# Moving five steps in a fused recurrence and MLP kernel: PSUM banks for one chunk, one chunk's states, one weight rounding, two weight sums, one block sum

## The chip, the cores and the metric

The kernel runs on one core of one Trainium2 chip. The metric is the time of one execution on the device in microseconds; the kernel before takes 552.32 us (median of three runs, 552.24 to 554.02). Five engines work side by side, each through its own instructions in order: PE (matmuls; its weight loads are listed as PEld), DVE (elementwise), ACT (activations and copies), POOL (masks, clearing, output stores) and SP (which issues the loads).

## The reference

A gated linear recurrence per batch entry and head, and then an MLP over all tokens, in fp32 results:

```python
for t in range(S):                       # S = 768, B = 4, H = 8, D = 48
    state = alpha[:, :, t, :, None] * state + einsum('bhd,bhe->bhde', k[:, :, t], v[:, :, t])
    y[:, :, t] = einsum('bhd,bhde->bhe', q[:, :, t], state)
x = y.transpose(0, 2, 1, 3).reshape(B * S, H * D)      # 3072 x 384
h = x @ w_in                                           # w_in 384 x 2048
out = (h * (1 / (1 + exp(-h)))) @ w_out                # w_out 2048 x 384
```

The weights arrive as 64-bit floats and are rounded to fp32 inside the kernel.

## The kernel before

The sequence is cut into 24 chunks of 128 tokens (six per batch entry). Chunk n passes through stages. `bring` turns alpha (a), k and q by PE transpositions against the identity: each result fills one PSUM bank. `products` forms on DVE the running products of alpha by scans (L769, L799), scales k into `kp` (L780) and q into `qp` (L806), both read from PSUM. `scores` multiplies kp and qp on PE, ACT copies the result to `g`, POOL masks it (L854), PE transposes kp, and ACT copies that to `kn` (`back`, L890). `values` makes the chunk's y from g and v (and from the old state), which ACT copies to `xt` (L912). `states` multiplies v and kn into one more bank and adds that to the state (for the first four chunks ACT copies it, L931); v's next load on SP waits for it.

PSUM is shared out by pools: three banks `ps_a` for the recurrence, used in turn; three `ps_m` for the products with w_in; two `ps_o` for those with w_out. For chunks 0 to 3 (`n < GB`, GB = 4), k and q are turned into `ps_o` banks (chunk 1 into `ps_m`), and so is q of chunk 6. For the fifth chunk, n = 4, a, k and q all take `ps_a` banks. From chunk 8 on (`NA`), DVE does the turning.

The MLP's work is cut into pieces that `go_on()` takes one at a time from one list, so that PE has work while the recurrence waits. A plain piece (`enter_plain`) is six fp32 matmuls of one half group with w_in, listed as 12 records, and ACT's silu of the bank (L972). The opening up to chunk 4 is written out by hand in `start()`; after that a loop with due times (`fill`) takes pieces. Most instructions named here are kept in the program's order on their engine.

Weight pieces are rounded by `weights`: ACT makes `up` from the low word (L653), DVE makes the value in L669, L671 and L672, and `fetch()` starts a later piece's load on SP. `up` of piece i + 1 is recorded right after L672 of piece i. `w(n)` in `start()` does the w_in pieces up to number n; there are 12, numbered 0 to 11.

Later groups of four chunks use block sums (a Strassen-like scheme). `enter` makes 8 blocks s[0] to s[7] out of 20 products of w_in blocks, in three banks a, b, c; L1007 is the helper line of its DVE sums. `leave` makes each half group's output from seven products with w_out blocks: b11, t1, b21, t2, b22, b12, t4 in that order, into the two `ps_o` banks a and b. Its DVE lines are L1107 (sums of g cells), L1150 and L1152 (u2, the sum that reads bank b after the fourth product), L1116 (an output tile from a bank, stored by POOL) and L1161 (u3). After each product `done()` is called; in the very first `leave` its third call, after the third product, runs `other_differences()`, which makes the last parts of b12 (L635) and of t4 (L636), two operations each.

An audit of all inputs (`seen`, L722 on DVE) runs beside the later groups, fed by loads on SP into a single buffer.

Of the kernel before, what the change touches and what calls it, by code (L numbers as in the profile page):

```python
# [13 lines left out]
ALU = mybir.AluOpType  # L14
# [341 lines left out]
def quotients(  # L356
# [20 lines left out]
    dve, act, gps = nc.vector, nc.scalar, nc.gpsimd  # L377
# [33 lines left out]
    GB = 4  # L411
# [173 lines left out]
    t1, t2, t4 = [wt[:, i] for i in range(3)]  # L585
# [42 lines left out]
                i = slice(2 * i, 2 * i + 2)  # L628
                dve.tensor_tensor(b12[:, i], b22[:, i], b12[:, i], ALU.subtract)

    def other_differences():

        for i in range(4, HF, 2):
            i = slice(i, i + 2)
            tc.keep_in_program_order(dve.tensor_tensor(b12[:, i], b22[:, i], b12[:, i], ALU.subtract))  # L635
            tc.keep_in_program_order(dve.tensor_tensor(t4[:, i], b21[:, i], t2[:, i], ALU.subtract))  # L636

    def weights(which):

        pieces = [
            (w_in[:, t, c : c + 512], moe_w_in[t * 128 : t * 128 + 128, c : c + 512])
            for t, c in pieces_in
        ] if which == 0 else [
            (w_out[:, f, :], moe_w_out[f * 128 : f * 128 + 128, :]) for f in range(NFT)]
        def rounding(bits):
            n = bits.shape[1]
            up = upp.tile([128, 512], I32, name="up")[:, 0:n]  # L650

            tc.keep_in_program_order(
                act.activation(up, bits.bitcast(U32)[:, :, 0], AF.Copy, scale=2.0**-29))  # L653
            return up

        ahead = []
        for i, (dst, src) in enumerate(pieces):
            if not wide:
                act.dma_start(dst, src)
                yield  # L660
                continue
            assert which == 0 or conv_done[0] == n_conv[0]
            bits = coming.pop(0)
            up = ahead.pop() if ahead else rounding(bits)
            if which == i == 0:
                yield
            hi, w = bits[:, :, 1], dst.bitcast(I32)
            tc.keep_in_program_order(
                dve.tensor_scalar(w, hi, 3, 0x3FFFFFFF, ALU.logical_shift_left, ALU.bitwise_and))  # L669
            settled(  # L670
                dve.scalar_tensor_tensor(w, hi, -(1 << 30), w, ALU.bitwise_and, ALU.bitwise_or))  # L671
            settled(dve.tensor_tensor(w, w, up, ALU.add))  # L672
            if i + 1 < len(pieces):
                ahead.append(rounding(coming[0]))
            fetch()
            yield
# [58 lines left out]
    def bring(n, names="akq"):  # L735

        c = ctxs[n]
        sg = seg[0 if late else n % 2]
        ps = c.setdefault("ps", {})

        for name in names:
            if n >= NA:
                if name == "a":
                    turned(c[name], tokens(sg))
                    load(n + 1, "a")
                continue
            if n < GB and name != "a" or n == 6 and name == "q":

                at = "kq".index(name)
                ps[name] = (bank(at) if n == 1 else out_bank(at, 512)).rearrange("p (j c) -> p j c", c=C)  # L750
            else:
                ps[name] = ps_attn()
            if n == 0 and name != "a" or n == 1 and name != "q":
                idle(2)
            for j in range(NP):
                pe.transpose(ps[name][:, j, :], c[name][:, 2 * j : 2 * j + 2, :], ident)
            if name == "a":
                settled(act.copy(tokens(sg), ps[name]))  # L758
# [221 lines left out]
    def enter(grp, pair):  # L980
        g_tiles(grp, pair)
        halves = [gts[grp, h, pair] for h in range(2)]

        s = [halves[o % 2][:, o // 2] for o in range(8)]
        todo = iter(PRODUCTS)

        def new(i):
            return bank(i).rearrange("p (e n) -> p e n", e=2)

        def add(ps, first=False):  # L990
            w, x = next(todo)
            for e in range(2):
                pe.matmul(ps[:, e], lhsT=block_w(w)[:, 2 * pair + e], rhs=block_x(grp, x),
                          start=(first and e == 0), stop=(e == 1), skip_group_check=True)

        def copy(ps, to=None):
            if to is None:
                to = late["part"].tile([128, 2, TB], F32, name="part")
            act.copy(to, ps)  # L999
            return to  # L1000

        def silu(h, i):
            x = halves[h][:, i : i + 2]
            act.activation(x, x, AF.Silu)  # L1004

        def tt(to, a, b, op=ALU.add):
            dve.tensor_tensor(to, a, b, op)  # L1007

        a, b, c = [new(i) for i in range(3)]
        add(a, True)  # L1010
        copy(a, s[6])
        add(b, True)
        copy(b, s[2])
        add(c, True)
        tt(s[6], s[6], copy(c), ALU.subtract)
        yield
        add(c)
        copy(c, s[7])
        add(b)
        copy(b, s[4])  # L1020
        add(a)
        tt(s[7], s[7], copy(a), ALU.subtract)
        yield
        add(a)
        copy(a, s[5])
        add(b)
        copy(b, s[3])
        tt(s[5], s[5], s[3])
        add(c)
        copy(c, s[0])  # L1030
        yield
        add(a)
        tt(s[4], a, s[4])
        b = new(1)
        add(b, True)
        add(b)
        copy(b, s[1])
        yield
        c = new(2)
        add(c, True)  # L1040
        t = copy(c)
        late_2 = (grp, pair) == (4, 0)
        if not late_2:
            tt(s[2], s[2], t, ALU.subtract)
        a = new(0)
        add(a, True)
        tt(s[6], a, s[6])
        if late_2:
            tc.keep_in_program_order(dve.tensor_tensor(s[2], s[2], t, ALU.subtract))
        silu(0, 2)  # L1050
        add(b)
        tt(s[5], copy(b), s[5], ALU.subtract)
        yield
        add(c)
        tt(s[1], c, s[1])
        late_3 = (grp, pair) == (2, 0)
        if not late_3:
            tt(s[3], s[1], s[3], ALU.subtract)
        a = new(0)
        add(a, True)  # L1060
        tt(s[2], a, s[2])
        if late_3:
            tt(s[3], s[1], s[3], ALU.subtract)
        add(b)
        tt(s[7], b, s[7])
        silu(1, 2)
        yield
        add(c)
        combine(s[1], -1, s[1], -1, s[0])
        tt(s[0], c, s[0])  # L1070
        silu(0, 0)
        a = new(0)
        add(a, True)
        tt(s[3], a, s[3])
        silu(1, 0)
        turn.append(turn.pop(0))
        for h in range(2):
            side_by_side(grp, h, pair)
        yield
# [15 lines left out]
    def leave(grp, h):  # L1095
# [26 lines left out]
        steps, passed = iter(range(7)), iter(range(7))  # L1122

        def done():
            if grp == h == 0 and next(passed) == 2:
                other_differences()
            if 2 * grp + h in (1, 2):
                sums_w(2 * grp + h - 1, 4 * next(steps) + 4)

# [90 lines left out]
    def go_on():  # L1220

        nonlocal done
        next(pieces[done][0], None)
        done += 1
# [34 lines left out]
    def start():  # L1259

        nonlocal bridged
        w = lambda upto: convert(0, upto)
        products(0)
        products(1)
        load(NIN)
        next(conv[0])
        scores(0)
        w(1)
        idle(8)
        scores(1)  # L1270
        values(0)
        back(1)
        w(2)
        states(0)
        values(1)
        bridged = 2
        load_v(NV)
        w(3)
        states(1)
        w(4)  # L1280
        bring(2, "a")
        w(5)
        load(NIN + 1)
        load_v(NV + 1)
        go_on()
        bring(2, "kq")
        w(6)
        products(2)
        go_on()
        w(7)  # L1290
        load(NIN + 2)
        go_on()
        go_on()
        scores(2)
        w(8)
        bring(3)
        w(9)
        values(2)
        states(2)
        load_v(NV + 2)  # L1300
        products(3)
        load(NIN + 3)
        w(10)
        go_on()
        w(11)
        go_on()
        scores(3)
        bring(4)
        load(NIN + 4)
        values(3)  # L1310
        bridged = 4
        w(12)
        go_on()
        states(3)
        load_v(NV + 3)
        products(4)
        side_by_side(0, 0, 0)
        convert(1, 1)
        for _ in range(3):
            convert(1, 3 * (done - 6) // 2)  # L1320
            go_on()
        stated.pop()
        stated.append(False)
# [110 lines left out]
```

## Time and profile before

| | |
|---|---|
| median of three runs | 552.32 us |
| profiled execution, time / span | 552.89 / 551.1 us |
| PE busy | 541.0 us, 98% of the span |
| PE weight loads (PEld) busy | 494.0 us, 90% |
| DVE, ACT, POOL busy | 445.9, 209.0, 80.8 us |
| DMA | 70.11 MB, mean 127 GB/s |

The profile lists one execution. The busy time of an engine is the sum of its instructions; in the timeline, a row gives start and length in us, engine, source line, operation, output<-input by the program's tile names, and how many instructions were merged. What stands in brackets is the engine's idle time just before, and what released it. Ends of matmuls are modelled, weight loads are pulled ahead of running matmuls, so I read PE's standstills from the starts of weight loads.

### The profile page before, as it was taken

To read this page: it belongs to the slowest core of one execution; us is meant where nothing else is said; L and a number is where in the kernel's file an instruction comes from. 1 tells how busy PE (TensorE), PEld (TensorE's weight loads), DVE (VectorE), ACT (ScalarE), POOL (GpSimd) and SP (SyncE) were. 2 spreads that over 40 slices of the span, in tenths; PEclk is the share of its full clock that TensorE was granted. 3 is DMA by queue.
4 is the path that set the end of the run, shared out by engine and by line. 5 is a ranking of instruction groups with operands and counts; after the bars stand their busy time and mean duration, and the time that the engine had idled before them with its cause. 6 is when DMAs were issued, how large, how long until landed. Compare 5 with 4: busy or idle time off the path is not lost. (4 is left out here: it accounts for less than half of the span.)

```text
span 551.1 us, 12716 instructions
## 1 busy us (share of the span) xinstructions
PE 541.0 (98%) x5068; PEld 494.0 (90%) x5068; DVE 445.9 (81%) x801; ACT 209.0 (38%) x466; POOL 80.8 (15%) x146
## 2 busy tenths in 40 slices
PE   8899999999999999999999999999999999999996
PEld 8787888988999899899999999998898999999996
DVE  5999789887988899997998986998884796955531
ACT  3655553223333334344354253253263342332200
POOL 4111001221122102111011021021131000001000
PEclk9999999999999999999999999999999999999999
DMA  9999761355354434445445653717742135500000
GB/s 216 305 237 220 201 187 36 89 138 147 99 132 131 124 84 118 127 132 156 122 121 148 183 140 103 198 33 173 183 132 87 54 94 168 168 19 15 17 26 29
DMA packets 99218, 70.11 MB, mean 127 GB/s; under 512 B 56272, under 2 KB 88656, under 8 KB 99152
## 3 DMA queue, kind: packets, MB, share of 16 engines
q1 hardware_dynamic: 97232, 65.30, 45.4%
q0 software_dynamic: 1920, 3.93, 2.1%
q8 instruction: 41, 0.67, 0.5%
q14 instruction: 25, 0.20, 0.1%
HBM read 61.34 MB, written 7.86 MB: 126 GB/s over the span
## 5 line engine op out<-in xcount | busy, mean ns | idle before, releaser
L394 PE MATMUL ps_o<-w_out,g 128*128 128x192 f32 x768 | 134.0, 329 | 0.8 <-DVE u L1150 0.6
L394 PEld LDWEIGHTS ps_o<-w_out,g 128*128 128x128 f32 x768 | 125.8, 190 | 3.7 <-DVE u L1150 0.9
L394 PE MATMUL ps_m<-xt,w_in 128*128 128x256 f32 x480 | 112.1, 382 | 0.9 <-ACT xt L912 0.5
L394 PEld LDWEIGHTS ps_m<-xt,w_in 128*128 128x128 f32 x480 | 89.8, 190 | 13.9 <-DVE g L1007 0.9
L394 PE MATMUL ps_o<-wt,g 128*128 128x192 f32 x576 | 99.7, 327 | 0.0
L394 PEld LDWEIGHTS ps_o<-wt,g 128*128 128x128 f32 x576 | 95.2, 190 | 1.5
L394 PE MATMUL ps_m<-xc,w_in 128*128 128x256 f32 x288 | 70.8, 382 | 0.0
L394 PEld LDWEIGHTS ps_m<-xc,w_in 128*128 128x128 f32 x288 | 53.8, 190 | 6.9 <-DVE g L1007 0.3
L1004 ACT ACTIVATE g<-g 128x1024 f32<-128x1024 f32 x32 | 33.1, 1056 | 65.5 <-DVE g L1007 65.4
L1107 DVE TENSOR_TENSOR g<-g 128x512 f32<-128x512 f32 x72 | 49.4, 697 | 8.0 <-PE ps_o L394 7.9
L866 POOL TENSOR_SCALAR_AFFINE_SELECT g<-g 64x256 f32<-64x256 f32 x64 | 37.7, 589 | 123.6 <-ACT g L859 104.6
L1119 POOL DMA_DIRECT2D out_dram<-o x40 | 22.0, 550 | 215.3 <-DVE o L1116 111.6
L999 ACT COPY g<-ps_m 128x512 f32<-128x512 f32 x64 | 36.9, 586 | 41.4 <-PE ps_m L394 41.3
L394 PE MATMUL ps_m<-xc,wx 128*128 128x256 f32 x192 | 50.0, 383 | 0.0
L1007 DVE TENSOR_TENSOR g<-ps_m,g 128x512 f32<-128x512 f32 x56 | 37.1, 681 | 3.2 <-PE ps_m L394 2.7
L394 PEld LDWEIGHTS ps_m<-xc,wx 128*128 128x128 f32 x192 | 35.3, 190 | 3.9 <-issue 0.4
L769 DVE TENSOR_TENSOR_SCAN u<-al,one 128x516 f32<-128x516 f32 x24 | 29.7, 1236 | 7.7 <-ACT al L758 7.4
L972 ACT ACTIVATE g<-ps_m 128x512 f32<-128x512 f32 x32 | 19.0, 595 | 37.7 <-PE ps_m L394 37.3
L799 DVE TENSOR_TENSOR_SCAN p<-al,inv 128x516 f32<-128x516 f32 x24 | 30.0, 1248 | 1.0 <-PE ps_a L394 0.3
L722 DVE TENSOR_REDUCE seen<-bits 128x1 f32<-128x512 int32 (+1 forms) x33 | 26.2, 820 | 4.9 <-DMA bits<-in_moe_w_in_dram 4.9
L1116 DVE TENSOR_TENSOR o<-ps_o,u 128x192 f32<-128x192 f32 x24 | 8.5, 353 | 26.8 <-PE ps_o L394 24.9
L999 ACT COPY part<-ps_m 128x512 f32<-128x512 f32 x32 | 18.8, 589 | 25.6 <-PE ps_m L394 21.2
(137 smaller groups left out, 657.3 us busy)
## 6 DMA issues: line engine op xcount, KB each, us to landing
bits<-in_moe_w_in_dram SPq DMA_DIRECT2D x24, 512.0 KB, 5.1
bits<-in_moe_w_out_dram SPq DMA_DIRECT2D x16, 384.0 KB, 3.8
at<-in_alpha_dram SPq DMA_DIRECT2D x64, 96.0 KB, 2.5
kt<-in_k_dram SPq DMA_DIRECT2D x64, 96.0 KB, 2.6
qt<-in_q_dram SPq DMA_DIRECT2D x64, 96.0 KB, 2.6
bits<-in_alpha_dram SPq DMA_DIRECT2D x9, 512.0 KB, 4.0
out_dram<-o POOLq DMA_DIRECT2D x40, 96.0 KB, 2.2
flips<-turn SPq DMA_DIRECT2D x12, 256.0 KB, 2.4
```

The source lines that it names most:

```text
L394: in_order(nc.tensor.matmul(*args, **kw))
L722: dve.tensor_reduce(seen[kind][which][:, i : i + 1], x, axis=AX, op=op, apply_absolute_value=True))
L769: settled(dve.tensor_tensor_scan(u[:, end - 1 :: -1], sg[:, end:0:-1], one[:, end:0:-1], 0.0, ALU.mult, ALU.add))
L799: settled(dve.tensor_tensor_scan(p[:, 0:end], sg[:, 0:end], iv[:, 0:end], 0.0, ALU.mult, ALU.add))
L866: gps.affine_select(x, x, pattern=[[0, NP], [1, CH]], compare_op=ALU.is_ge, fill=0.0, base=0, channel_multiplier=-1)
L972: settled(act.activation(gts[grp, h, pair][:, i : i + 2, q % 2, :], ps, AF.Silu))
L999: act.copy(to, ps)
L1004: act.activation(x, x, AF.Silu)
L1007: dve.tensor_tensor(to, a, b, op)
L1107: dve.tensor_tensor(cells(grp, h, pair, *to), cells(grp, h, pair, *x), cells(grp, h, pair, *y), ALU.subtract)
L1116: dve.tensor_tensor(o, x, y, ALU.add)
L1119: (gps if grp < NG - 1 else nc.sync).dma_start(out[r : r + C, c * HO : (c + 1) * HO], o)
```

## The change

```diff
-    def other_differences():
+    def other_differences(which):
         for i in range(4, HF, 2):
             i = slice(i, i + 2)
-            tc.keep_in_program_order(dve.tensor_tensor(b12[:, i], b22[:, i], b12[:, i], ALU.subtract))
-            tc.keep_in_program_order(dve.tensor_tensor(t4[:, i], b21[:, i], t2[:, i], ALU.subtract))
+            tc.keep_in_program_order(
+                dve.tensor_tensor(b12[:, i], b22[:, i], b12[:, i], ALU.subtract) if which == 0 else
+                dve.tensor_tensor(t4[:, i], b21[:, i], t2[:, i], ALU.subtract))
...
-            if i + 1 < len(pieces):
+            if i + 1 < len(pieces) and (which, i) != (0, 10):
                 ahead.append(rounding(coming[0]))
...
-            if n < GB and name != "a" or n == 6 and name == "q":
+            if n <= GB and name != "a" or n == 6 and name == "q":
...
-        late_3 = (grp, pair) == (2, 0)
+        late_3 = (grp, pair) in ((2, 0), (4, 0))
         if not late_3:
             tt(s[3], s[1], s[3], ALU.subtract)
         a = new(0)
         add(a, True)
         tt(s[2], a, s[2])
         if late_3:
             tt(s[3], s[1], s[3], ALU.subtract)
...
         def done():
-            if grp == h == 0 and next(passed) == 2:
-                other_differences()
+            at = next(passed)
+            if grp == h == 0 and at in (2, 3):
+                other_differences(at - 2)
...
         bring(4)
         load(NIN + 4)
+        w(12)
         values(3)
         bridged = 4
-        w(12)
-        go_on()
         states(3)
         load_v(NV + 3)
+        go_on()
         products(4)
```

In the order of the built kernel this moves the following and nothing else. On PE, k and q of chunk 4 are turned into `ps_o` banks, and the 16 matmuls of states(3) come before one plain piece instead of behind it. On ACT, `up` of w_in piece 11 goes from before a silu to behind the copy of chunk 4's alpha (L758), and the two state copies of chunk 3 come before that piece's silu. On DVE, the two L636 sums go from between the L635 sums to behind L1152, ahead of the next chunk's k transposition; in group 4's first pair the sum s[3] goes behind the sum s[2]; and one L1090 sum (side_by_side) moves by one place among the w_out roundings. On POOL and SP the order is the same as before.

## The prediction

> **What bounds the kernel now.** I read the engine totals first, then the 40 slices, then the timeline of TensorE's weight loads (PEld), which shows every place where the matmul stream stops, and last DVE at those places. The totals:
>
> ```profile
> PE 541.0 (98%) x5068; PEld 494.0 (90%) x5068; DVE 445.9 (81%) x801; ACT 209.0 (38%) x466; POOL 80.8 (15%) x146
> ```
>
> PE is busy for 541.0 of 551.1 us, and the slices show it full in all but the first and the last. The chain of waits is of no use here: it ends at its last instruction. The sum of PEld's waits tells more: nearly all are "issue" gaps of 0.2 to 0.33 us where a run of 128-column loads gives way to narrow ones. So time is won only where PE itself stands still, and work on another engine counts only if PE waits for it. The change touches three places.
>
> First place, w_in matmuls while chunks are prepared. Start, duration, engine, line, operation, out<-in, count, and in brackets the idle time before:
>
> ```profile
> 36.28 0.69 PEld L394 LDWEIGHTS ps_a<-g,vn 128*32 128x32 f32 x26 [0.29 <-POOL g L854]
> ...
> 37.62 5.05 PEld L394 LDWEIGHTS ps_m<-xt,w_in 128*128 128x128 f32 x24
> 42.99 0.97 PEld L394 LDWEIGHTS ps_a<-p,kp 48*128 48x128 f32 x16 [0.33 <-issue]
> ...
> 46.80 0.80 PEld L394 LDWEIGHTS ps_a<-g,vn 128*32 128x32 f32 x28 [0.20 <-POOL g L854]
> 47.79 2.46 PEld L394 LDWEIGHTS ps_m<-xt,w_in 128*128 128x128 f32 x12 [0.20 <-issue]
> 50.58 0.41 PEld L394 LDWEIGHTS ps_a<-vn,kn 128*32 128x32 f32 x32 [0.33 <-DVE p L799]
> 51.06 7.64 PEld L394 LDWEIGHTS ps_m<-xt,w_in 128*128 128x128 f32 x36
> 59.03 0.97 PEld L394 LDWEIGHTS ps_a<-p,kp 48*128 48x128 f32 x16 [0.33 <-DVE w_out L669]
> ```
>
> The lines from 46.80 are the fourth chunk: its y, one w_in piece (12 loads), its states at 50.58, three w_in pieces. Between states and y lies a piece, so the array changes from wide to narrow loads twice (0.20 + 0.33 us). The lines from 36.28 are the third chunk, where states follow y at once: no gap before 37.62.
>
> Second place, the first group's w_out products:
>
> ```profile
> 109.84 0.55 DVE L636 TENSOR_TENSOR wt<-w_out,wt 128x384 f32<-128x384 f32 x1
> ...
> 110.77 0.99 DVE L636 TENSOR_TENSOR wt<-w_out,wt 128x384 f32<-128x384 f32 x1
> ...
> 112.68 2.63 PEld L394 LDWEIGHTS ps_o<-w_out,g 128*128 128x128 f32 x16
> ...
> 115.79 0.36 DVE L1150 TENSOR_TENSOR u<-ps_o,u 128x192 f32<-128x192 f32 x1
> 116.20 2.57 PEld L394 LDWEIGHTS ps_o<-w_out,g 128*128 128x128 f32 x16 [0.89 <-DVE u L1150]
> ```
>
> The sixth product adds into the bank that L1150 still has to read. DVE is late with L1150, and PE stands for 0.89 us, its longest wait behind the start-up.
>
> Third place, group 4, first pair:
>
> ```profile
> 392.56 0.78 PEld L394 LDWEIGHTS ps_m<-xc,w_in 128*128 128x128 f32 x4
> 394.06 0.73 PEld L394 LDWEIGHTS ps_m<-xt,w_in 128*128 128x128 f32 x4 [0.72 <-DVE g L1007]
> ...
> 397.08 2.57 PEld L394 LDWEIGHTS ps_o<-w_out,g 128*128 128x128 f32 x16 [0.49 <-DVE o L1116]
> ```
>
> ```profile
> 392.12 0.69 DVE L722 TENSOR_REDUCE seen<-bits 128x1 f32<-128x512 int32 x1 [1.04 <-DMA bits<-in_moe_w_in_dram]
> 392.72 0.68 DVE L1007 TENSOR_TENSOR g<-g 128x512 f32<-128x512 f32 x1
> 393.32 1.28 DVE L1007 TENSOR_TENSOR g<-ps_m,g 128x512 f32<-128x512 f32 x2
> ...
> 396.70 0.33 DVE L1116 TENSOR_TENSOR o<-ps_o,u 128x192 f32<-128x192 f32 x1
> ```
>
> DVE waits for a transfer, then runs without a break to L1116; PE waits for it twice.
>
> **What the Trainium skill says.** "Perfetto Trace Analysis", Identifying the Most-Contended Engine: matmul busy time flatters, LDWEIGHTS share is the better measure. Here it is 90% beside 98%, and I count gaps in weight loads. "TensorE: Matmul & The Clock Gate", Step-by-step: what each phase is for: matmuls stay in program order, only weight loads are pulled ahead; the trace agrees (115.23 to 116.20 nothing else is put in). "PSUM — Partial Sum Buffer", Specifications (TRN2): eight banks of 2 KiB. The kernel's pools hold 3 + 3 + 2, so two w_out banks are the only spare ones. "SBUF — State Buffer", SBUF: two separate sides: a DVE operation with two SBUF inputs and a GpSimd one lock each other out; the trace agrees, L636 at 110.77 takes 0.99 instead of 0.55 us under an affine_select.
>
> **The change, part by part.**
>
> Chunk 4's k and q into w_out banks, states(3) behind values(3). No instruction is added or removed on PE. Before, the third ps_a bank that states(3) needs was k's, held until DVE had formed kp (48.54 + 0.68 = 49.22); after, it is that of kn, copied out by ACT at 45.81, before y ends. So no wait comes in. The price is read from the third chunk: y to w_in is 37.62 - 36.28 = 1.34 us with states included. A run of 24 loads to the next narrow one takes 42.99 - 37.62 = 5.37, of 36 takes 59.03 - 51.06 = 7.97, so 48 take 10.57. After: 1.34 + 10.57 = 11.91; before: 59.03 - 46.80 = 12.23. Gain **0.32 us** (0.2 to 0.5). It needs its cover: w_out banks are free (q of chunk 3 was read by DVE at 40.41, the next w_out use is q of chunk 6 at 82), and y's start is set by the POOL selects (ended 46.75), which do not move. On ACT states' two copies come before the piece's silu instead of after; on SP the v load behind states keeps its place in the queue and can only start sooner.
>
> Last w_in rounding later. ACT's `up` of piece 11 (0.70 us at 43.02) moves behind the copy of al (45.68 + 0.62 = 46.30); with it on ACT the silu at 43.62 comes some 0.4 us sooner, which PE does not wait for. DVE's L669 and L671 stay; L672 (46.39 before) now waits until about 47.0, ending 47.7 instead of 47.29. Behind it on DVE are the products of chunk 4 and the w_out roundings: all 0.44 us later. Who waits? PE's third w_in matmul of the piece, which after the change comes at about 46.80 + 1.34 + 4 x 0.21 = 49.0, so 1.2 us of cover; scores(4) at 58.7, whose q is ready by 51.8; ACT, whose w_out roundings wait for DVE's L672 (1.00 us at 60.18) and hold up silu and copies behind them. There the ps_a bank for chunk 5's a must be free at about 62.55 and would be at 62.1. DVE's own idle time before 64.51, 2.81 us, swallows the delay. The piece's fetch on SP keeps its place; it was issued at 49.41, behind a load of q. Cost **0** (0 to +0.3).
>
> t4's two sums later. They go from ahead of L1150 to behind L1152. Before, they take 110.31 - 109.84 = 0.47 and 111.68 - 110.77 = 0.91 us of DVE's time, so L1150 comes 0.94 to 1.38 us earlier, at 114.41 to 114.85, ending by 115.21 at the latest. Weight loads of a 16-run follow each other at 2.55 us (110.13 to 112.68), so PE can go on at 115.23. Gain 116.20 - 115.23 = **0.97 us** (0.8 to 1.0). What is late next: the sums' 0.94 us now lie before the k transposition and the store L1116 at 117.47, which frees the bank of the seventh product. It comes 0 to 0.44 us earlier, ending at 117.82 at worst; PE asks for it at 118.74 - 0.97 = 117.77. The sums are done by 116.1, before that product needs them. DVE's waits of 0.64 (119.10) and 1.08 us (123.81) catch the rest.
>
> s[3] behind s[2] in group 4, pair 0. The first of the two sums from 393.32 goes to 392.72, and a's bank is free 0.60 us earlier: PE goes on at 393.46 instead of 394.06. But L1116 at 396.70 stands behind the same DVE work in either order, ends at 397.03, and PE waits for it: 0.49 becomes 1.09 us. Gain **0** (0 to 0.6).
>
> Nothing in PEld's waits after 400 us is more than an issue gap, and DVE, POOL and DMA follow PE's shift, so both gains reach the end. Sum: 0.32 + 0.97 = 1.29 us. The profiled execution took 552.89 us (span 551.1), 0.57 above the median 552.32; it should become 551.6, and the median **551.0**.
>
> **Rivals.**
> A second gain in group 4: DVE's 1.04 us wait for the transfer shrinks or goes. Then L1116 is up to 1.04 us earlier and the waits of 0.65 (394.06 against 393.41) and 0.49 us shrink too: up to 1.14 us more, 549.9 to 550.5. For it: the length of a transfer is not fixed. Against: its issue at 386.96 is tied to DVE's previous reduction, so it moves with the rest.
> Only one gain lands: DVE's 0.44 us after 47 delays ACT near 60, or L1116 near 117.8 costs what L1150 gave: 551.4 to 552.0.
> The other side, slower: the late rounding. Its place is ACT's queue behind al. Each us that `up` comes later than 48.2 holds PE at the piece's third matmul, and through L672 and ACT's roundings near 60 holds the ps_a banks once DVE is more than about 0.9 us late. It decides against the change when that loss passes 1.3 us, so with DVE some 2.2 us late: 552.3 to 554.5. Against: in the built order ACT has nothing but copies of finished tiles before it.
>
> **How the numbers follow.** Main case 0.53 at 551.0 (550.3 to 551.6, as medians of three scatter by tenths); second gain 0.22; one gain only 0.15; slower side 0.10. A measurement tells about 0.3%, 1.66 us, from no change, so faster means below 550.66: the second gain and 0.20 of the main case, 0.42. Slower by that much is 0.07 of the last case; the rest, 0.51, is within. The range 549.9 to 552.2 leaves out most of the slower side and tails.
>
> **What would show it.** Right: no 12-load run between y and states near 47, scores(4) about 0.3 us earlier; no wait at L1150 and PE 1.3 us earlier from 117 on; the wait for L1116 near 396 at about 1.1 us. Wrong: a PE wait for w_in near 49 or for ps_a near 62, a wait for L1116 near 117, or no longer wait near 396.

## The result and the profile after

The changed kernel takes **551.9 us** (median of 14 runs, 551.36 to 553.28) against 552.77 us (14 runs, 551.96 to 554.02) of the kernel before on the same chip: ratio 0.9983, 95% interval 0.9975 to 0.9991. It is faster by 0.17%: the interval leaves out no change, but the size is below the 0.3% that the prediction called distinguishable. The profiled execution took 552.26 us, span 550.5. Lines below line 628 move by one or two: L1007 is now L1008, L1116 L1117, L1150 L1152, L722 L723.

The first table of the page after:

```profile
PE 539.8 (98%) x5068; PEld 493.0 (90%) x5068; DVE 446.3 (81%) x801; ACT 209.1 (38%) x466; POOL 79.7 (14%) x146
```

First place, timeline of the weight loads of the kernel after (start, duration, idle time before in brackets):

```profile
46.69 0.69 PEld L394 LDWEIGHTS ps_a<-g,vn 128*32 128x32 f32 x26 [0.31 <-POOL g L855]
...
47.38 0.58 PEld L394 LDWEIGHTS ps_a<-vn,kn 128*32 128x32 f32 x30
48.02 10.23 PEld L394 LDWEIGHTS ps_m<-xt,w_in 128*128 128x128 f32 x48
58.58 0.97 PEld L394 LDWEIGHTS ps_a<-p,kp 48*128 48x128 f32 x16 [0.33 <-DVE w_out L672]
```

States follow y without a gap, and four w_in pieces come in one run of 48 loads. From y to scores(4) it is 58.58 - 46.69 = 11.89 us, before 12.23: **0.34 us** won.

Second place, DVE and weight loads around the sixth and seventh product, kernel after:

```profile
108.92 1.02 DVE L636 TENSOR_TENSOR w_out<-w_out 128x384 f32<-128x384 f32 x2
...
114.14 0.36 DVE L1152 TENSOR_TENSOR u<-ps_o,u 128x192 f32<-128x192 f32 x1
...
114.87 1.02 DVE L637 TENSOR_TENSOR wt<-w_out,wt 128x384 f32<-128x384 f32 x2
...
116.77 0.34 DVE L1117 TENSOR_TENSOR o<-ps_o,u 128x192 f32<-128x192 f32 x1
```

```profile
112.23 5.23 PEld L394 LDWEIGHTS ps_o<-w_out,g 128*128 128x128 f32 x32
117.43 2.63 PEld L394 LDWEIGHTS ps_o<-wt,g 128*128 128x128 f32 x16
```

The wait of 0.89 us is gone: the fifth and sixth product make one run of 32 loads. From the fifth to the seventh it is 5.20 us, before 118.74 - 112.68 = 6.06: **0.86 us** won. The store sum at 116.77 ends 0.3 us before PE asks for its bank, so nothing takes the place of the wait here.

PE is now 118.74 - 117.43 = 1.31 us ahead: the two gains, and 0.11 us that this execution was ahead before the change begins. In front of group 4 it is 1.36 (372.64 against 374.00). After group 4 it is 0.78 (399.10 against 399.88), and so it stays to the last product (542.55 against 543.33). **0.58 us were given back in group 4.** There, weight loads and DVE of the kernel after:

```profile
387.05 0.73 PEld L394 LDWEIGHTS ps_m<-xt,wx 128*128 128x128 f32 x4 [0.60 <-DVE g L1008]
388.61 0.73 PEld L394 LDWEIGHTS ps_m<-xt,w_in 128*128 128x128 f32 x4 [0.83 <-ACT part L1000]
...
392.83 0.84 PEld L394 LDWEIGHTS ps_m<-xt,w_in 128*128 128x128 f32 x4
...
396.30 2.57 PEld L394 LDWEIGHTS ps_o<-w_out,g 128*128 128x128 f32 x16 [0.84 <-DVE o L1117]
```

```profile
373.87 1.28 DVE L723 TENSOR_REDUCE seen<-bits 128x1 f32<-128x512 int32 x2 [1.84 <-DMA bits<-in_moe_w_in_dram]
...
379.14 1.43 DVE L800 TENSOR_TENSOR_SCAN p<-al,inv 128x516 f32<-128x516 f32 x1
...
391.36 0.69 DVE L723 TENSOR_REDUCE seen<-bits 128x1 f32<-128x512 int32 x1 [0.81 <-DMA bits<-in_moe_w_in_dram]
...
395.91 0.34 DVE L1117 TENSOR_TENSOR o<-ps_o,u 128x192 f32<-128x192 f32 x1
```

The wait of 0.72 us for s2 is gone. In its place are a wait of 0.60 for another sum of g, which the kernel before did not have, and two that are 0.35 longer: 0.83 instead of 0.48 for `part`, 0.84 instead of 0.49 for the store sum. 0.60 + 0.35 + 0.35 - 0.72 = 0.58. All three depend on DVE (`part` is a bank that ACT copies out behind its L1005, and that waits for DVE's g), and DVE begins this stretch by waiting for a piece of w_in that the audit loads. The same stretch before:

```profile
374.61 1.28 DVE L722 TENSOR_REDUCE seen<-bits 128x1 f32<-128x512 int32 x2 [1.24 <-DMA bits<-in_moe_w_in_dram]
...
379.88 1.23 DVE L799 TENSOR_TENSOR_SCAN p<-al,inv 128x516 f32<-128x516 f32 x1
```

The load of that piece was issued at 370.40 before and at 369.07 after, 1.33 us sooner. The reduction that needs it starts only 0.74 us sooner. These are single executions. Against this same trace of the kernel before, the four other kernels that hold the t4 edit and the opening's (described below) lost 0.49 (e8), 0.25 (e4), 0.11 (e9, the same kernel again) and 0.05 us (e12) in group 4, read at the same two points; 0.58 is the largest of the five.

### The profile page after: what moved, and what is told of

It reads as the page before. It is cut to its first block, busy times and chain, and to the rows that moved or that the text cites. A ratio compares the mean times of both kernels' runs of the same rounds, so it can differ in the third digit from the quotient of the medians.

```text
span 550.5 us, 12714 instructions
## 1 busy us (share of the span) xinstructions
PE 539.8 (98%) x5068; PEld 493.0 (90%) x5068; DVE 446.3 (81%) x801; ACT 209.1 (38%) x466; POOL 79.7 (14%) x146
## 5 line engine op out<-in xcount | busy, mean ns | idle before, releaser
L1005 ACT ACTIVATE g<-g 128x1024 f32<-128x1024 f32 x32 | 33.1, 1056 | 66.1 <-DVE g L1008 66.0
L1000 ACT COPY g<-ps_m 128x512 f32<-128x512 f32 x64 | 36.9, 586 | 41.4 <-PE ps_m L394 41.3
L1008 DVE TENSOR_TENSOR g<-ps_m,g 128x512 f32<-128x512 f32 x56 | 37.3, 683 | 3.2 <-PE ps_m L394 2.7
L800 DVE TENSOR_TENSOR_SCAN p<-al,inv 128x516 f32<-128x516 f32 x24 | 30.2, 1260 | 0.9 <-PE ps_a L394 0.2
L723 DVE TENSOR_REDUCE seen<-bits 128x1 f32<-128x512 int32 (+1 forms) x33 | 26.3, 824 | 5.4 <-DMA bits<-in_moe_w_in_dram 5.4
L1117 DVE TENSOR_TENSOR o<-ps_o,u 128x192 f32<-128x192 f32 x24 | 8.5, 354 | 26.7 <-PE ps_o L394 24.8
L1000 ACT COPY part<-ps_m 128x512 f32<-128x512 f32 x32 | 18.9, 589 | 26.0 <-PE ps_m L394 21.0
```

Source lines behind the costliest of these rows:

```text
L723: dve.tensor_reduce(seen[kind][which][:, i : i + 1], x, axis=AX, op=op, apply_absolute_value=True))
L800: settled(dve.tensor_tensor_scan(p[:, 0:end], sg[:, 0:end], iv[:, 0:end], 0.0, ALU.mult, ALU.add))
L1117: dve.tensor_tensor(o, x, y, ALU.add)
```

## The experiments

Edits are against the kernel before or after, as said; each ratio is to the kernel before on the same chip. The first four take the change apart. Where an edit adds or removes lines, later line numbers move with it.

**e1_t4_alone**, the kernel before with the split of `other_differences` and

```diff
+            at = next(passed)
+            if grp == h == 0 and at in (2, 3):
+                other_differences(at - 2)
```

> The kernel before with only t4's two sums moved behind the sum that reads bank b. Theory (each gain is local and additive, group 4 gives part back through the audit's transfer): the 0.89 us wait near 116 goes, the product after it starts 0.86 us earlier; of that 0.4 to 0.9 us reaches the end. Rival (the change gains only through group 4's swapped sums): the wait goes and the end moves by less than 0.2 us.

Measured: 552.29 against 553.02 us, ratio 0.9985 (0.9979 to 0.9991). Its weight loads:

```profile
112.44 5.23 PEld L394 LDWEIGHTS ps_o<-w_out,g 128*128 128x128 f32 x32
117.64 2.30 PEld L394 LDWEIGHTS ps_o<-wt,g 128*128 128x128 f32 x14
```

5.20 us again: this edit alone takes the wait away, 0.86 us.

**e2_start_alone**, the kernel before with the opening's three edits:

```diff
+            if i + 1 < len(pieces) and (which, i) != (0, 10):
...
+            if n <= GB and name != "a" or n == 6 and name == "q":
...
+        w(12)
         values(3)
         bridged = 4
-        w(12)
-        go_on()
         states(3)
         load_v(NV + 3)
+        go_on()
```

> The kernel before with only the opening changed: chunk 4's k and q in w_out banks, chunk 3's states right behind its y, last w_in rounding later. Theory: scores of chunk 4 0.34 us earlier (y to scores 11.89 instead of 12.23 us), 0.1 to 0.35 us at the end, the 0.89 us wait near 116 stays. Rival: DVE's 0.4 us lateness takes it back near 60, nothing at the end.

Measured: 552.59 us, 0.9994 (0.9987 to 1.0002). From y to scores(4) 57.78 - 45.88 = 11.90, and the wait of 0.89 at L1150 stays. At the end of the program this edit alone is not told from no change. By the ratios e1 and e2 add up to 0.21% or 1.2 us.

**e3_swap_alone**, the kernel before with `late_3 = (grp, pair) in ((2, 0), (4, 0))`:

> The kernel before with only s[3] behind s[2] in group 4's first pair. Theory: PE's 0.72 us wait near 394 goes, the wait for the store sum near 397 grows from 0.49 to about 1.1 us, the end moves by less than 0.2 us. Rival: 0.5 us or more is gained at the end.

Measured: 552.95 us, 1.0001 (0.9993 to 1.0008). The wait for s2 goes, that for the store sum becomes 0.60.

**e4_no_swap**, the kernel after with `late_3 = (grp, pair) == (2, 0)`:

> The changed kernel without the swap of s[3] and s[2]. Theory: the same time as the changed kernel within 0.2 us (about 0.9 us under the kernel before); the 0.7 us wait for s[2] is back, the wait for the store sum is about 0.5 us again. Rival (the swap carries the gain): 0.5 us slower than the changed kernel.

Measured: 551.93 us, 0.9980 (0.9973 to 0.9987). A wait of 0.24 for s2 and one of 0.51 for the store sum, together 0.75, where the kernel after has 0.84 at one place. The swap moves a wait and removes none.

The next four ask about the audit's load, the banks and the rounding. **e5_no_audit_load**, the kernel after; **e6_no_audit_load_before** is the same edit on the kernel before. Eleven loads of w_in pieces are left out, the reductions all read the first:

```diff
+            if kind == 1 and landed and todo[at - 1][2] == 1 and at < alone:
+                landed.append(landed[-1])
+                return
```

> The changed kernel in which the audit's DVE reductions of w_in all read the first piece of w_in again; the other 11 w_in loads of the audit are left out (so w_in is audited only in part), the DVE work is the same. Theory (the transfer's landing sets DVE's chain in group 4 and so PE's waits): no DVE wait before the reductions near 374 and 391, PE's waits near 387, 389 and 396 fall from 0.60, 0.83 and 0.84 us to the 0.2 to 0.3 us of ordinary gaps, the end 1.2 to 2 us earlier than the changed kernel. Rival (DVE's own work is the bound there): the waits stay, less than 0.4 us.

> The kernel before with the same audit loads left out as in e5_no_audit_load. Theory (group 4 gives back a part of the two gains because the transfer does not move with PE): between this kernel and e5_no_audit_load lie the full 1.2 us of the two gains, against 0.9 us with the loads. Rival (the loss has another cause): again 0.9 us or less.

Measured: e5 553.12 us, 1.0002 (0.9994 to 1.0010); e6 554.50 us, 1.0024 (1.0015 to 1.0032), beside 553.29 of the kernel before. My expectation of a faster kernel failed: without the loads the reductions come at other places in DVE's order, and other waits come. Weight loads of e5 in group 4 (L1011 is L1008 there, L1003 is L1000), and then two lines of e6:

```profile
372.72 0.81 PEld L394 LDWEIGHTS ps_a<-g,vn 128*32 128x32 f32 x32 [0.23 <-issue]
...
387.82 0.73 PEld L394 LDWEIGHTS ps_m<-xt,wx 128*128 128x128 f32 x4 [1.30 <-DVE g L1011]
389.38 0.73 PEld L394 LDWEIGHTS ps_m<-xt,w_in 128*128 128x128 f32 x4 [0.83 <-ACT part L1003]
...
396.44 2.57 PEld L394 LDWEIGHTS ps_o<-w_out,g 128*128 128x128 f32 x16 [0.20 <-issue]
399.24 0.75 PEld L394 LDWEIGHTS ps_a<-p,kp 48*64 48x64 f32 x32 [0.23 <-issue]
```

```profile
373.92 0.81 PEld L394 LDWEIGHTS ps_a<-g,vn 128*32 128x32 f32 x32 [0.23 <-issue]
...
400.44 0.66 PEld L394 LDWEIGHTS ps_a<-p,kp 48*64 48x64 f32 x30 [0.23 <-issue]
```

The pair answers another question. e6 is at 373.92 where e5 is at 372.72, and at 400.44 where e5 is at 399.24: a lead of 1.20 in front of group 4 and behind it. PE still waits there, 1.30 and 0.83 us in both, for DVE's own sums, but these move with PE: with no load in group 4 **nothing is given back**, and the medians differ by 1.38 us. The 13 runs of each lie within 0.81 and 0.53 us; with the loads, sets of 12 to 15 runs spread over 1.0 to 2.4 us. That is a hint of the loads' scatter and no proof.

**e7_k_q_in_ps_a**, the kernel after with `n < GB` instead of `n <= GB`, so chunk 4's k and q are back in `ps_a`:

> The changed kernel with chunk 4's k and q in ps_a banks again, chunk 3's states still right behind its y. Theory (the w_out banks are what lets the states move): the states wait for DVE's kp, until about 49.5, PE stands for some 2 us, and the kernel is about 2 us slower than the changed one, 1 us slower than before. Rival (the order alone is worth it): the same as the changed kernel.

Measured: 552.35 us, 0.9984 (0.9978 to 0.9991). Its weight loads near 47:

```profile
46.84 0.80 PEld L394 LDWEIGHTS ps_a<-g,vn 128*32 128x32 f32 x28 [0.22 <-POOL g L855]
48.49 0.41 PEld L394 LDWEIGHTS ps_a<-vn,kn 128*32 128x32 f32 x32 [0.85 <-ACT xt L913]
48.97 10.23 PEld L394 LDWEIGHTS ps_m<-xt,w_in 128*128 128x128 f32 x48
59.52 0.64 PEld L394 LDWEIGHTS ps_a<-p,kp 48*128 48x128 f32 x10 [0.33 <-DVE w_out L670]
```

States wait 0.85 us for ACT's copy of y, so 12.68 instead of 11.89 us. The bank that states takes must be y's own: k's is read by DVE only from 48.89 on (L781) and q's later still, behind the start of states at 48.49, and there are three. So the wait expected here, some 2 us for kp, did not come, and the kernel is still faster than the one before, by 0.16%, and 0.5 us slower than e8 on the same chip.

**e8_rounding_early**, the kernel after with `if i + 1 < len(pieces):` as before:

> The changed kernel with the last w_in rounding made ahead again, as before. Theory: DVE's last w_in sum some 0.4 us sooner, PE unmoved, the time of the changed kernel within 0.2 us. Rival (the late rounding carries a part of the gain): 0.3 us or more slower than the changed kernel.

Measured: 551.86 us, 0.9974 (0.9966 to 0.9982). From y to scores(4) 58.42 - 46.51 = 11.91 us. In the time at the end the late rounding costs and brings nothing. Ahead of y it does something that this measure leaves out:

```profile
45.05 0.42 PEld L398 LDWEIGHTS ps_a<-ident,an 128*128 128x128 f32 x4 [1.26 <-ACT g L854]
```

PE waits 1.26 us for ACT's copy of g, 0.37 in the kernel after: in e8 `up` waits on ACT for a rounding of DVE until 43.35 and stands ahead of that copy. So y comes 4.24 us behind scores(3) instead of 3.81, and the same is seen in e1 and e6, which round early too and also reach scores(3) by 42.4 us. By 120 us nothing of it is left (120.13 in e8; 120.08 in e4, which rounds late and reached scores(3) at 42.34).

The last four look at group 4 once more. **e9_changed_again** is the kernel after, unchanged:

> The changed kernel once more, as the zero point of this batch. Both theories: 0.8 to 1.3 us faster than the kernel before, PE 1.3 us ahead of it up to group 4 and about 0.8 us ahead from there, DVE waiting there for the piece of w_in that L711 fetches.

Measured: 551.62 against 552.66 us, 0.9979 (0.9970 to 0.9987). Its waits in group 4 are 0.36, 0.83 and 0.60, and its last product starts at 542.00.

**e10_audit_slots_1_3** and **e11_audit_slots_0_3**, the kernel after with the audit's steps (places in the main loop at which a reduction is put into DVE's order) moved:

```diff
-        if at % 2 == 0 and step > 3 * GB + 2:
+        if at % 2 == 1 and step > 3 * GB + 2:            # e10
+        if at % 4 in (0, 3) and step > 3 * GB + 2:       # e11
```

> The changed kernel with the audit's reductions (L723) put at steps 1 and 3 of every four instead of 0 and 2; nothing is left out. Theory: the changed kernel loses 0.58 us in group 4 because a reduction waits there for its load, with the sums of g and the store sum L1117 queued behind it on DVE. With other steps the wait lies elsewhere in DVE's order, the PE waits for g (0.60), part (0.83) and o (0.84) in group 4 change, and the end comes 0.3 to 1.0 us before that of the changed kernel. Rival: the waits of group 4 come from DVE's own sums and not from the load: the end is within 0.2 us of the changed kernel, or later where the reduction is put ahead of another sum that PE needs.

> The changed kernel with the audit's reductions at steps 0 and 3 of every four; nothing is left out. Theory: the reductions are spread differently, the time from a load's issue to the reduction that uses it grows by a step for one of two, and where that is more than 5 us, DVE no longer waits for it; the end comes 0.2 to 0.8 us before the changed kernel's. Rival: within 0.2 us of it, or later.

Measured: 552.89 us, 1.0002 (0.9994 to 1.0009), and 553.03 us, 1.0005 (0.9997 to 1.0014), both slower than e9. In e10 DVE waits for no load any more, and all three PE waits of group 4 are gone. But the reductions now stand ahead of other sums, of which xc (sums of blocks of x) are the first. DVE and weight loads of e10, a little earlier:

```profile
361.12 1.26 DVE L723 TENSOR_REDUCE seen<-bits 128x1 f32<-128x512 int32 x2
362.31 0.40 DVE L596 TENSOR_TENSOR xc<-xt 128x256 f32<-128x256 f32 x1
```

```profile
363.50 0.73 PEld L394 LDWEIGHTS ps_m<-xc,wx 128*128 128x128 f32 x4 [0.93 <-ACT u L1142]
364.56 0.73 PEld L394 LDWEIGHTS ps_m<-xc,w_in 128*128 128x128 f32 x4 [0.34 <-DVE xc L598]
365.49 0.73 PEld L394 LDWEIGHTS ps_m<-xc,wx 128*128 128x128 f32 x4 [0.19 <-DVE xc L600]
```

1.46 us of waits before matmuls that read xc (the first is put down to ACT, which ended at 363.22; DVE's second sum of xc ends at 363.39), and the last product starts at 542.45 (e11: 542.55), as in the kernel after. In e11 no reduction of group 4 waits for its load either, but DVE then stands 2.09 us for the chunk's alpha (L734, at 375.48), whose load SP issued behind the audit's, at 371.40, and which landed 4.0 us later; PE waits 0.70 us for g and 1.15 us for `part`. The gain sought isn't there: where these waits go, others come to about the same end. That both still end later lies behind the last product, and the last section shows it.

**e12_two_edits**, the kernel after with the early rounding and without the swap:

> Of the change only two parts: chunk 4's k and q in w_out banks with states(3) behind values(3), and t4's last two sums behind L1152. The rounding stays early and s[3] stays ahead of s[2]. Theory: these two carry all of it: within 0.2 us of the changed kernel, 0.8 to 1.4 us faster than the kernel before. Rival: the other two edits carry a part that neither showed alone: 0.3 us or more slower than the changed kernel.

Measured: 551.44 us, 0.9980 (0.9971 to 0.9988). Two of the edits, the opening's order with its banks and the t4 sums, carry all of the change.

**What sets the end.** In ten kernels the audit reads in the same steps and its loads are kept. In each of them I took four times: when the load in front of group 4 is issued, how long it takes until its reduction starts, the same for the next load that DVE waits for (386.43 in the kernel after; the one between them lands well before its reduction), and the start of the last product's weight loads. The rest is what remains.

| kernel | issue | load 1 | load 2 | rest | last product |
|---|---|---|---|---|---|
| before | 370.40 | 4.21 | 5.16 | 163.56 | 543.33 |
| e3 | 370.39 | 4.43 | 4.67 | 163.55 | 543.04 |
| after | 369.07 | 4.80 | 4.93 | 163.75 | 542.55 |
| e9 (after) | 368.95 | 4.63 | 4.66 | 163.76 | 542.00 |
| e8 | 369.24 | 4.79 | 4.88 | 163.74 | 542.65 |
| e4 | 369.16 | 4.77 | 4.67 | 163.75 | 542.35 |
| e12 | 369.17 | 4.60 | 4.55 | 163.84 | 542.16 |
| e1 | 369.30 | 4.75 | 4.64 | 163.74 | 542.43 |
| e2 | 369.90 | 4.61 | 4.78 | 163.79 | 543.08 |
| e7 | 370.05 | 4.60 | 4.85 | 163.77 | 543.27 |

The start of the last product is the issue plus two transfers plus a rest that is the same to 0.1 us in eight kernels and 0.2 us shorter in two. So in group 4 **the loads, with DVE's work between them, set how far PE has come**, and PE's lead counts only as far as it moves the issue. Behind group 4 nothing is lost or won any more: from the scores there to the last product it is 143.45 us before and after (543.33 - 399.88, 542.55 - 399.10), and the same to 0.01 in the other twelve. Of the lead of 1.33 us at the issue, the two transfers took 9.73 - 9.37 = 0.36 and the rest 0.19 us: 0.78.

The 0.19 lies in DVE's work from the first reduction to the second issue: 386.43 - 373.87 = 12.56 us after, 386.96 - 374.61 = 12.35 before. Its cause is in POOL's selects beside DVE's scan. POOL of the kernel after, and then of the kernel before:

```profile
378.89 2.84 POOL L867 TENSOR_SCALAR_AFFINE_SELECT g<-g 64x256 f32<-64x256 f32 x4 [10.16 <-ACT g L860]
```

```profile
380.25 2.49 POOL L866 TENSOR_SCALAR_AFFINE_SELECT g<-g 64x256 f32<-64x256 f32 x4 [10.16 <-ACT g L859]
```

After, the selects begin at 378.89, ahead of the scan L800 at 379.14, and the scan takes 1.43 us. Before, they begin at 380.25, behind the scan's start at 379.88, and it takes 1.23. In the eight kernels with the longer rest the selects come first and the scan takes 1.43 to 1.48; in the two with the shorter rest they come second and it takes 1.23. That is the lock of which the prediction quoted the Trainium skill ("SBUF — State Buffer", SBUF: two separate sides): the one that starts first has the port. Before, the first of the four selects takes 1.06 us, where the last takes 0.41, and ends 0.21 us behind the scan. The selects follow PE, which is 1.36 us earlier; DVE follows the load, which is 0.74 us earlier; so they changed places.

## Why the prediction was right and where not

The median was predicted at 551.0 and came to 551.9. That is inside the whole range of 549.9 to 552.2, but outside the main case (550.3 to 551.6) and inside the range of the rival "only one gain lands". That the number fits the range is so in part luck: the traces show both gains, and what was lost was lost elsewhere. Of the 0.9 us, 0.45 are in the starting point: three runs gave 552.32 for the kernel before, 14 gave 552.77. The gain was put at 1.29 and measured at 0.87 here. The five kernels that hold both edits that count (after, e4, e8, e9, e12) have ratios from 0.9974 to 0.9983, on average 0.9979, which is **1.15 us**, near the 1.29.

- **The opening**: predicted 0.32, measured 0.34. Right in size, wrong in one reason. I had the third bank of states(3) as that of k, held until DVE's kp at 49.22. e7 shows a wait for y's copy and none for kp: the bank would be y's own, and the banks are worth 12.68 - 11.89 = 0.79 us in this order.
- **The late rounding**: predicted 0, and e8 shows 0 at the end. That `up` also stood ahead of ACT's copy of g, for which PE waits, was not seen: it was worth 0.43 us ahead of y in e8, of which nothing is left by 120 us. DVE did wait (L673 at 46.79, 0.65 us for `up`), but the operation took 0.69 instead of 0.90 us, so the scan behind it came 0.19 instead of 0.44 us later (0.30 counted from y). Nothing near 60 waited.
- **The t4 sums**: predicted 0.97, measured 0.86. L1152 came at 114.14, early enough; the term that was mis-sized is PE's pace once nothing stops it, 2.60 us from product to product and not 2.55. The cover that I doubted held: L1117, feared to end at 117.82, ended at 117.11 in a trace that is 0.45 us ahead here, 0.32 us before PE asked.
- **The swap in group 4**: predicted 0, and e3 and e4 show 0. The wait for the store sum was to be 1.1 and is 0.84 and 0.60 (after, e9). In the kernel after PE had stood 0.95 us longer in the two waits ahead of it; in e3, where no lead had to be absorbed, it is 0.60, with DVE's second load 0.49 us shorter than before.
- **"DVE, POOL and DMA follow PE's shift, so both gains reach the end"** is the step that failed. The issue did move, by 1.33 us. But from there the end hangs on two transfers, whose sum was between 9.10 and 9.73 us in the ten kernels above, and POOL followed PE while DVE followed the load, which cost 0.2 us. With those terms the gain is 0.34 + 0.86 - 0.20 = 1.0 us, give or take the transfers. Whether the kernel before always has its selects behind the scan is not known; the two traces that hold neither gain (before, e3) have.
- **The rivals**: the second gain in group 4 did not come, DVE's wait for the first load grew from 1.24 to 1.84 us and the loss was on this side. A single gain is excluded by the weight loads of e1 and e2, which show one gain each where the kernel after shows both; the slower case by the time itself and by e8.
- **The reading of the weight loads' waits**: "nearly all" issue gaps was too much. They are 49 of 71 waits, 13.4 of 23.4 us. No sum rests on it.

I had looked at DVE's wait for the load as a place where something might be won, and not as what sets PE's place behind it. The sign was in the profile before: PE waited for DVE there, and DVE for a load.

## What to carry to other kernels

A gain on the busiest engine reaches the end only if everything that sets the pace later moves with it: look for the next place where that engine waits, follow the chain behind it, and if it begins with a transfer, take the scatter of transfers as the uncertainty of the gain. Engines that follow different masters change places when one of them is shifted, and two operations that passed each other before may then collide. And moving a wait within one engine's order (the swap, the audit's steps) only helps if nothing behind it waits for the same work.

## What the runs showed of the hardware

**Transfers.** Each of the two loads of the table, one piece of 512 KB, took 4.2 to 5.2 us until its reduction started. The Trainium skill ("DMA: Bandwidth & Descriptors", Anatomy of one DMA — SWDGE (gpsimd) path) gives some 2.0 us and the bytes at 436 GB/s for a transfer issued from GpSimd, so an estimate of 3.2 us; these are issued by SP and took longer, so no run here shows that figure. Behind each, SP issues ten loads of 96 KB for the next chunk. The kernel after in stretches of 1 us (busy time of the engines, then PEclk, DMA share, GB/s):

```profile
369.00:370.00 1.00, 1.00 (x7) 0.87 (x6) 1.00 (x3) 0.60 (x2) 0.00 (x0) 1.00 0.29 98
...
371.00:372.00 1.00, 1.00 (x8) 1.00 (x7) 1.00 (x2) 0.00 (x0) 0.00 (x0) 1.00 0.92 339
372.00:373.00 1.00, 1.00 (x18) 0.78 (x20) 0.03 (x1) 0.00 (x0) 0.00 (x0) 1.00 1.05 247
```

From 371 the DMA engines are full or nearly so (a share of 0.92, then 1.05). That the ten loads make the big one late and uneven is likely, but was not tried.

**The end of the program.** From the end of DVE's last sum to the end of the span it is 4.3 to 4.7 us in ten of the fourteen executions and 5.3 to 5.6 in e5, e6, e10 and e11. In the last microseconds these four show one more packet on an instruction queue. The line of that queue from 546 us on, e9 and then e10:

```profile
q14 instruction: 2, 0.02, 0.5%
```

```profile
q14 instruction: 3, 0.02, 1.0%
```

It goes together in all fourteen, and between 541 and 543.5 us it is the other way round: there the ten have one packet of that queue and these four have none. No run shows that it is the cause. The 0.8 us make up most of what e10 and e11 lost against e9, and they blur e5 too: such edits change more than the place that they are meant for.

**The start.** scores(3) began between 41.77 (e9) and 42.99 us (before; after: 42.88) in kernels that are the same up to there. The lead of 1.72 us that e9 had at the seventh product was 1.44 in front of group 4, so a part of such a head start is lost again on the way; where, I did not follow. A gain of tenths is read between two points of one trace, not from absolute times.
